# Weight sums by negation and accumulating loads, and a two-level down product in two more chunks

## The chip, the core and the metric

The kernel runs on one core of a Trainium2 chip. The core has a matrix engine (TensorE, PE in the profile; PEld are its weight loads), a vector engine (VectorE, DVE), a scalar engine (ScalarE, ACT), a general engine (GpSimd, POOL) and a queue engine (SyncE, SP) that only issues transfers here. Transfers that SP and POOL issue run on 16 DMA engines. The metric is the device time of one execution in microseconds (us); lower is better.

## The reference

An attention block without softmax, followed by a mixture of four experts. For each of 8 batches and 8 heads of width 64, `kv = k^T v`, then `q kv`, then each row is divided by its root mean square and multiplied by `g_norm`. The heads are put side by side, which gives x with 4608 rows (tokens) of 512. Then:

```
p = domain_probs / (domain_probs.sum(-1, keepdims=True) + 1e-09)
for e in range(4):
    h = np.maximum(x @ w1[e], 0.0)          # 4608x512 @ 512x1024
    out += p[:, e:e + 1] * (h @ w2[e])      # 4608x1024 @ 1024x512
```

Everything is float32. Nearly all of the work is in the eight large products of the experts.

## The kernel before

**Tiling.** The tokens are cut into 9 chunks of 512: eight are the first 512 rows of each batch, the ninth holds the remaining 64 rows of all eight. The loops run over expert e (0 to 3) and within it over chunk c (0 to 8); stage s = 9 e + c. Each stage has an *up* product (x by w1, then ReLU) and a *down* product (hidden by w2).

**Fewer products.** Both products use the scheme of Strassen and Winograd: a matrix is cut into 2 by 2 blocks, and 7 block products replace 8, at the price of sums of blocks before and after. `up` applies it twice, one inside the other: 7 outer by 7 inner products of 128-wide blocks. It does so for every stage but the first. For the down product there are two forms:

- `down` (line 1077) applies the scheme once: 2 token halves, 7 products, and 4 blocks of depth for each, 256 columns wide (matmul at line 1095). A product is scaled by the token's probability and merged into an accumulator straight from PSUM (lines 1042, 1049).
- `down_deep` (line 1117) applies it twice: 7 outer by 7 inner products, 2 blocks of depth each, 128 columns wide (matmul at line 1170). It needs sums of the hidden blocks (three for each outer product, through `combine`, line 360), evictions and sums of the inner products (lines 1198, 1206), and sums of the outer ones (line 1236) before the merge.

A float32 matmul shows as two instructions. Expert 0 uses `down` throughout. Experts 1 to 3 use `down_deep` for chunks 0 to 7, and `down` for chunk 8.

**Weights.** Both weights of an expert are loaded as four 512 KB blocks each, of 128 partitions by 1024. `weights_1` (line 417) forms four more blocks by sums, 5 = 21 + 4, 6 = 5 - 1, 7 = 1 - 21, 3 = 2 - 6, and then for each of the 7 outer factors four inner sums of 128 by 256 (kept in `w1y`). `weights_2` (line 466) forms 5 = 12 - 1, 6 = 3 - 5, 7 = 3 - 12, 4 = 2 - 6; its `inner` makes four sums for each outer factor into `w2y`. These serve `down_deep` only. The seven `w2y` slots are memory that the attention block used before (`kv`, `kvbd`, `x_rem`), and the profile shows them under those names. A sum is one `tensor_tensor` at line 360, on DVE or on POOL, whichever the planner picks.

**Memory.** Whole blocks of 128 by 1024 (weights, hidden blocks, products, accumulators) live in 29 slots named `big`, with 4 more (`small` in the profile) once the attention block is done. PSUM has 8 banks: `u1` and `u2` for up, `db` and `ab` for down.

**Order.** Nothing is left to a run-time scheduler. Every operation is handed to a planner with a key, in units of one stage, and a cost for each engine that may run it; the planner (`Plan.layout`, line 81) simulates the engines with these costs and gives each engine a fixed list. PE and SP take the first operation that is ready in order of key; the others take the ready one that is due first. A slot is given out when the planner starts the operation that first writes it. A transfer that POOL issues is taken to land 5.5 us after its issue (line 175). `port` (lines 129, 176) keeps `combine` sums from being planned on DVE and POOL at the same time. For the next expert's weights the keys are given at lines 1292 to 1294, where s is the last stage of the expert: loads of w1 from s, its inner sums from s + 0.3 and its four block sums at s + 0.55 to s + 0.8; loads of w2 from s + 0.6, its block sums from s + 1.0, its inner sums from s + 1.3. The up of stage s has keys s to s + 1, its down s + 1.2 to s + 2.2.

The results of experts 1 to 3 are added to the output in memory by transfers that accumulate, which POOL issues (line 1065); the last stage reads the output back instead.

Of the kernel before, what the change touches and what calls it, by code (L numbers as in the profile page):

```python
# [10 lines left out]
ALU = mybir.AluOpType  # L11
# [23 lines left out]
class Plan:  # L35
# [45 lines left out]
    def layout(self, slots, later, idle, idle_banks, idle_until):  # L81
# [51 lines left out]
        while left:  # L133
# [4 lines left out]
            for eng in todo:  # L138
                if busy[eng] > t:
                    continue  # L140
                pending = todo[eng]
                while pending and pending[0].start is not None:
                    pending.pop(0)
                if not pending:
                    continue
                reach = pending[0].key + self.REACH[eng]
                best = None
                for op in pending:
                    if op.key > reach:
                        break  # L150
                    if op.start is not None:
                        continue
                    if best is not None and op.due >= best.due:
                        continue
                    when = ready(op, eng)
                    if when is None:
                        continue
                    if when > t:
                        heapq.heappush(wake, when)
                        continue  # L160
                    best = op
                    if eng in ("PE", "SP"):
                        break
                if best is not None:
                    op = best
                    op.start, op.eng = t, eng
                    if eng == "SP":
                        busy[eng] = t + op.cost[eng]
                        bus = max(bus, t + 1.5) + op.kb / 215.0
                        op.end = bus + 0.5  # L170
                        lanes = lanes[1:] + [op.end]
                    else:
                        op.end = busy[eng] = t + op.cost[eng]
                        if op.kb:
                            op.end += 5.5
                    if op.port:
                        port = op.end
                        heapq.heappush(wake, port)
                    for b in op.outs:
                        if b.kind is not None and b.slot is None:  # L180
                            free[b.kind].sort()
                            b.slot = free[b.kind].pop(0)[1]
                            b.ap = slots[b.kind][b.slot]
                    for b in op.bufs:
                        b.left -= 1
                        if b.left == 0 and b.kind is not None:
                            end = max(o.end for o in [op] + b.readers + b.writers) + self.CROSS
                            free[b.kind].append((end, b.slot))
                            live[b.kind] -= 1
                            ended[b.kind] = max(end, ended.get(b.kind, 0.0))  # L190
                            for rule in [r for r in later if not any(live.get(k) for k in r[0])]:
                                later.remove(rule)
                                end = max(ended[k] for k in rule[0])
                                for ap in rule[2]:
                                    free.setdefault(rule[1], []).append((end, len(slots[rule[1]])))
                                    slots[rule[1]].append(ap)
                                heapq.heappush(wake, end)
                    heapq.heappush(wake, busy[eng])
                    heapq.heappush(wake, op.end + self.SAME)
                    heapq.heappush(wake, op.end + self.CROSS)  # L200
                    order.append(op)
                    left -= 1
                    moved = True
                if eng == "PE" and busy[eng] <= t and 1.6 <= t and front < idle_until:
                    kind, spare = next((
                        (k, f) for k in idle_banks for f in free[k] if f[0] <= t
                    ), (None, None))
                    if spare is not None:
                        op = Op(front, {"PE": 0.23}, None, (), (), 0, False)
                        op.start, op.eng, op.end = t, eng, t + 0.23  # L210
                        op.fn = lambda eng, bank=slots[kind][spare[1]]: idle(bank)
                        busy[eng] = op.end
                        free[kind].remove(spare)
                        free[kind].append((op.end, spare[1]))
                        heapq.heappush(wake, op.end)
                        order.append(op)
                        moved = True
# [13 lines left out]
def kernel(  # L231
# [110 lines left out]
    def act(n):  # L342
        return {"ACT": 0.155 + 0.00088 * n}
# [69 lines left out]
    def w2_src(e, uh, dh):  # L413
        rows = moe_w2[e][uh * HF:(uh + 1) * HF, dh * HN:(dh + 1) * HN]
        return rows.rearrange("(kt p) d -> p kt d", p=P)

    def weights_1(e, key, step, need):

        f = {n: Buf("big", f"w1_{e}_{n}") for n in (1, 2, 21, 4, 5, 6, 7, 3)}
        corner = {}  # L420
        w1corner[e] = {}
        for i, (n, dh, uh) in enumerate(((1, 0, 0), (2, 1, 0), (21, 0, 1), (4, 1, 1))):
            corner[n] = Buf(None, f"w1c_{e}_{n}")
            w1corner[e][uh, dh] = f[n], corner[n]
            load(
                key + i * step, f[n],
                lambda n=n: f[n].ap[:].rearrange("p (k u) -> p k u", k=2),
                w1_src(e, dh, uh), 512, also=[corner[n]],
            )

        def form(k_, o, a, b, op):
            corner[o] = Buf(None, f"w1c_{e}_{o}")
            combine(
                k_, either(1024), lambda: f[o].ap[:], lambda: f[a].ap[:], lambda: f[b].ap[:], op,
                [f[a], f[b], corner[a], corner[b]], [f[o], corner[o]],
            )

        def sums():
            form(need + 0.25, 5, 21, 4, ALU.add)
            form(need + 0.26, 6, 5, 1, ALU.subtract)  # L440
            form(need + 0.5, 7, 1, 21, ALU.subtract)
            form(need + 0.5, 3, 2, 6, ALU.subtract)
            w1f[e] = {}
            for j, m in enumerate(OUTER):
                x, low, y = f[m], corner[m], Buf("w1y", f"w1y_{e}_{m}")
                parts = {}
                for n, (uq, kt) in ((1, (0, 0)), (2, (0, 1)), (7, (1, 0)), (4, (1, 1))):
                    parts[n] = (
                        [x, low] if n == 7 else [x],
                        lambda x=x, uq=uq, kt=kt: two(x.ap[:])[:, kt, uq * HN:(uq + 1) * HN],  # L450
                    )
                for n, at in ((5, 0), (6, 1), (3, 2)):
                    parts[n] = ([y], lambda y=y, at=at: y.ap[:, at * HN:(at + 1) * HN])
                for o, a, b, op in (
                    (5, 7, 4, ALU.add), (7, 1, 7, ALU.subtract), (6, 5, 1, ALU.subtract),
                    (3, 2, 6, ALU.subtract),
                ):
                    combine(
                        need + j / 7, either(HN), parts[o][1], parts[a][1], parts[b][1], op,
                        parts[a][0] + parts[b][0], [low] if o == 7 else [y],  # L460
                    )
                w1f[e][m] = parts

        return sums

    def weights_2(e, key, step, deep):
# [9 lines left out]
        def form(k_, o, a, b, op):  # L476
            combine(
                k_, either(1024), lambda: f[o].ap[:], lambda: f[a].ap[:], lambda: f[b].ap[:], op,
                [f[a], f[b]], [f[o]],
            )  # L480

        form(key + 4 * step, 5, 12, 1, ALU.subtract)
        form(key + 5 * step, 6, 3, 5, ALU.subtract)
        form(key + 6 * step, 7, 3, 12, ALU.subtract)
        form(key + 7 * step, 4, 2, 6, ALU.subtract)
        w2f[e] = f

        def inner():
# [798 lines left out]
    for e in range(E):  # L1287
        for c in range(NCH):
# [1 line left out]
            if e == 0 and c + 1 < B:  # L1290
                attention(c + 1, s - 0.1, 0.8, s + 0.5)
            if e + 1 < E and c == NCH - 1:
                weights_1(e + 1, s + 0.0, 0.12, s + 0.3)()
                inner[e + 1] = weights_2(e + 1, s + 0.6, 0.1, s + 1.3)
            if s + 1 < E * NCH:
                if e == 0 and c + 1 < NCH:
                    x_views[s + 1] = x_forms(c + 1, s + 0.7)
# [3 lines left out]
                up(s, e, x_views.pop(s))  # L1301
            if c == 0 and e:
                inner[e]()
            if e and c < NCH - 1:
                if not primed:
                    banks = [Buf("ab", f"prime{i}") for i in range(2)]

# [66 lines left out]
```

## Time and profile before

| | us |
|---|---|
| median of 4 runs | 1730.39 (1729.66 to 1730.51) |
| the profiled execution | 1730.5 |
| its span | 1728.7 |
| L881, `up`, matrix instructions on `xf` and `big`: 3104, mean | 0.275 |
| L1095, `down`: instructions on `db`: 1120, mean | 0.381 |
| plain loads of the expert weights, 512 KB each: issue to landing | 4.8 (median) |
| accumulating output transfers, 256 KB each: issue to landing | 5.6 (median) |

Matrix instructions overlap, so the mean duration of one is longer than the interval between two; the interval is read from the chain of waits, where a run of n instructions has its length beside it. The last stage of expert 1 is s = 17; its down runs between 907 and 956 us, and expert 2 repeats the pattern 396 us later.

### The profile page before, as it was taken

The page shows a single profiled execution, that of the slowest core. Times are in us where ns is not written, and L with a number is a line of the kernel's source. Part 1 is how long each engine was busy: PE and PEld are TensorE (multiplying, and loading weights), DVE is VectorE, ACT ScalarE, POOL GpSimd, SP SyncE. Part 2 cuts the span into 40 slices and gives each one's busy share as a digit, 9 for nine tenths or more (in the row PEclk, how much of TensorE's full clock was granted, in tenths as well). Part 3 has the DMA queues.
Part 4 walks back from the last instruction along what each step waited for, and adds up shares of the span by engine and source line. Part 5 has one row for each costly group of instructions (what it writes and reads, how often), then busy time and mean ns, then how long its engine had stood idle before and what let it go on. Part 6 is the DMA issues. An engine that isn't in the chain of part 4 may idle for free.

```text
span 1728.7 us, 38444 instructions
## 1 busy us (share of the span) xinstructions
PE 1719.3 (99%) x15334; PEld 1651.5 (96%) x15334; DVE 1225.9 (71%) x1969; ACT 938.4 (54%) x2300; POOL 614.2 (36%) x560
## 2 busy tenths in 40 slices
PE   9999999999999999999999999999999999999998
PEld 7699999999999999999999999999999999999998
DVE  4755655565676777777788877777788877777774
ACT  3354544454444565656555556666655566565652
POOL 2421322133334333333345333333345333333331
PEclk9999999999999999999999999999999999999999
DMA  9756444633433243444465344444475344444432
GB/s 239 219 161 193 151 121 132 193 135 125 151 128 100 94 115 104 115 107 112 130 187 111 99 110 111 111 111 110 108 208 113 98 111 111 111 111 103 114 103 49
DMA packets 148596, 220.94 MB, mean 128 GB/s; under 512 B 49600, under 2 KB 90816, under 8 KB 148416
## 3 DMA queue, kind: packets, MB, share of 16 engines
q1 hardware_dynamic: 133312, 191.21, 35.2%
q0 software_dynamic: 15104, 27.27, 10.7%
q8 instruction: 120, 1.97, 0.5%
q14 instruction: 60, 0.49, 0.1%
HBM read 145.30 MB, written 73.14 MB: 126 GB/s over the span
## 4 chain that ended last, share of the span: by engine, by line
PE 99%; POOL 0%; DVE 0%; ACT 0%; issue 0%; POOLq 0%
PE u L881 45%; PE db L1170 19%; PE db L1095 14%; PE ab L1170 12%; PE ab L1095 2%; PE u L968 2%; PE ab L634 1%; PE ab L678 1%; PE ab L620 1%; PE ab L1323 1%; PE ab L660 1%; PE u L1095 1%; PE db L660 0%; POOL rt L551 0%; PE ab L722 0%; PE ab L704 0%
## 5 line engine op out<-in xcount | busy, mean ns | idle before, releaser
L360 DVE TENSOR_TENSOR big<-big,big 128x1024 f32<-128x1024 f32 (+1 forms) x450 | 442.3, 996 | 34.9 <-ACT big L864 23.8
L881 PE MATMUL u<-xf,big 128*128 128x128 f32 x3104 | 453.0, 275 | 0.0
L881 PEld LDWEIGHTS u<-xf,big 128*128 128x128 f32 x3104 | 401.3, 192 | 2.2
L881 PE MATMUL u<-xf,w1y 128*128 128x128 f32 x2652 | 389.6, 275 | 0.0
L908 DVE TENSOR_TENSOR big<-u,snap 128x256 f32<-128x256 f32 x430 | 181.4, 422 | 234.3 <-PE u L881 175.5
L881 PEld LDWEIGHTS u<-xf,w1y 128*128 128x128 f32 x2652 | 343.4, 192 | 2.2
L900 ACT ACTIVATE snap<-u 128x256 f32<-128x256 f32 x490 | 187.8, 383 | 251.5 <-PE u L881 212.7
L1095 PE MATMUL db<-big,big 128*128 128x256 f32 x1120 | 265.3, 381 | 2.1 <-DVE big L560 2.1
L1095 PEld LDWEIGHTS db<-big,big 128*128 128x128 f32 x1120 | 203.5, 191 | 24.8 <-DVE big L560 2.3
L900 ACT ACTIVATE big<-u 128x256 f32<-128x256 f32 x430 | 164.7, 383 | 110.6 <-PE u L881 74.5
L360 POOL TENSOR_TENSOR big<-big,big 128x256 f32<-128x256 f32 (+1 forms) x138 | 170.1, 1239 | 132.4 <-DVE big L360 49.4
L1170 PE MATMUL db<-big,big 128*128 128x128 f32 x1056 | 146.7, 275 | 0.0
L864 ACT ACTIVATE big<-big 128x1024 f32<-128x1024 f32 x128 | 134.5, 1050 | 2.7 <-POOL big L360 1.5
L1170 PEld LDWEIGHTS db<-big,big 128*128 128x128 f32 x1056 | 132.1, 192 | 0.1
L1236 POOL TENSOR_TENSOR big<-big 128x512 f32<-128x512 f32 x26 | 33.0, 1269 | 269.0 <-DVE big L360 263.9
L1198 ACT ACTIVATE snap<-db 128x256 f32<-128x256 f32 x192 | 68.4, 356 | 100.0 <-PE db L1170 95.1
L360 POOL TENSOR_TENSOR big<-big 128x512 f32<-128x512 f32 (+1 forms) x57 | 70.3, 1233 | 126.8 <-DVE big L360 102.6
L1170 PE MATMUL db<-kv,big 128*128 128x128 f32 x804 | 114.6, 275 | 0.0
L1065 POOL DMA_DIRECT2D out_dram<-big x100 | 91.2, 988 | 48.2 <-ACT snap L1198 22.8
L900 ACT ACTIVATE u<-u 128x256 f32<-128x256 f32 x245 | 90.9, 371 | 28.1 <-PE u L881 8.0
L1170 PEld LDWEIGHTS db<-kv,big 128*128 128x128 f32 x804 | 102.1, 192 | 0.1
L1206 DVE TENSOR_TENSOR big<-ab,snap 128x256 f32<-128x256 f32 x140 | 59.1, 422 | 56.8 <-ACT snap L1198 31.8
(218 smaller groups left out, 2686.6 us busy)
## 6 DMA issues: line engine op xcount, KB each, us to landing
xf<-x SPq DMA_DIRECT2D x108, 512.0 KB, 3.6
out_dram<-big POOLq DMA_DIRECT2D x84, 256.0 KB, 5.6
xf<-x_h SPq DMA_DIRECT2D x81, 256.0 KB, 3.0
xf<-x SPq DMA_DIRECT2D x81, 256.0 KB, 3.1
x<-xf SPq DMA_DIRECT2D x36, 512.0 KB, 6.6
big<-in_moe_w_dram SPq DMA_DIRECT2D x25, 512.0 KB, 4.8
small<-in_q_dram SPq DMA_DIRECT2D x72, 128.0 KB, 4.9
kv<-in_k_dram SPq DMA_DIRECT2D x30, 288.0 KB, 4.8
```

Of the source, the lines that this page charges most:

```text
L360: lambda eng: adder(eng).tensor_tensor(out=out_(), in0=a(), in1=b(), op=op),
L864: lambda eng: nc.scalar.activation(out=b.ap[:], in_=b.ap[:], func=ACT.Relu),
L881: nc.tensor.matmul(ps.ap[:, u * P:(u + 1) * P], lhsT=w1f[e][m][mm][1]()[:, u * P:(u + 1) * P], rhs=views[m][mm][1](), start=(mm in (1, 5) ...
L900: lambda eng: nc.scalar.activation(out=where(), in_=ps.ap[:, 0:HN], func=ACT.Copy),
L908: lambda eng: nc.vector.tensor_tensor(out=block(whole, a, t), in0=src.ap[:, 0:HN], in1=add_.ap[:], op=ALU.add),
L968: nc.tensor.matmul(bank.ap[:], lhsT=two(w.ap[:])[:, kt, ut * P:(ut + 1) * P], rhs=two(xh[dh].ap[:])[:, kt, :], start=(dh == kt == 0), stop ...
L1065: nc.gpsimd.dma_start(out=dst, in_=cell(i)[parts, :], accum_op=ALU.add)
L1095: nc.tensor.matmul(ps.ap[:, 0:HN], lhsT=four(h[m])[:, kt // 2, t, kt % 2, :], rhs=w2f[e][m].ap[:, kt * HN:(kt + 1) * HN], start=(m in (1, ...
L1170: nc.tensor.matmul(ps.ap[:, o * P:(o + 1) * P], lhsT=b.ap[:, col:col + P], rhs=w2q[e][m][mm][1]()[:, kt, :], start=(mm in (1, 5) and o == ...
L1198: lambda eng: nc.scalar.activation(out=where(), in_=group_of(ps.ap), func=ACT.Copy),
L1206: lambda eng: nc.vector.tensor_tensor(out=cell(tq, dq), in0=group_of(src.ap), in1=group_of(add_.ap), op=ALU.add,),
L1236: lambda eng: adder(eng).tensor_tensor(out=whole(to), in0=whole(a), in1=whole(b), op=ALU.add),
```

## The change

Three things are done.

1. For experts 1 to 3, two of the four block sums of w1 (7 and 3) and all four of w2 (5, 6, 7, 4) are made in another way. ACT writes the negated block into the new slot (a Copy with scale -1, 128 by 1024), and then a transfer that POOL issues adds the other operand to it, straight from the weights in DRAM: 7 = -21 + block 1, 3 = -6 + block 2; 5 = -1 + block 12, 6 = -5 + block 3, 7 = -12 + block 3, 4 = -6 + block 2. The w1 transfers read 256 rows of 2 KB, the w2 ones 512 rows of 1 KB. Expert 0 keeps the sums. The sums 5 and 6 of w1 stay as they were.
2. The last chunks of experts 1 and 2 (stages 17 and 26) use `down_deep` in place of `down`. Only expert 0 and the very last stage keep `down`.
3. The planner takes these 512 KB transfers to land 9.0 us after their issue. The keys for the next expert's weights move: inner sums of w1 from s + 0.3 to s + 0.6 (its block sums with them), loads of w2 from s + 0.6 to s + 1.0 (its block sums with them), inner sums of w2 from s + 1.3 to s + 1.45. These keys hold for all three changes of expert.

```diff
@@ Plan.layout
                         if op.kb:
-                            op.end += 5.5
+                            op.end += 9.0 if op.kb == 512 else 5.5
@@ new, after w2_src
+    def subtract_from(key, to, view, a, src, reads, writes):
+
+        plan.add(
+            key, act(2 * NT),
+            lambda eng: nc.scalar.activation(
+                out=to.ap[:], in_=a.ap[:], func=ACT.Copy, scale=-1.0),
+            reads=reads, writes=[to],
+        )
+        plan.add(
+            key, {"POOL": 1.0},
+            lambda eng: nc.gpsimd.dma_start(out=view(to.ap), in_=src, accum_op=ALU.add),
+            reads=[to], writes=writes, kb=512,
+        )
@@ weights_1
+        def from_dram(k_, o, a, dh, uh):
+            corner[o] = Buf(None, f"w1c_{e}_{o}")
+            subtract_from(
+                k_, f[o], lambda ap: ap[:].rearrange("p (k u) -> p k u", k=2), f[a],
+                w1_src(e, dh, uh), [f[a], corner[a]], [f[o], corner[o]],
+            )
+
         def sums():
             form(need + 0.25, 5, 21, 4, ALU.add)
             form(need + 0.26, 6, 5, 1, ALU.subtract)
-            form(need + 0.5, 7, 1, 21, ALU.subtract)
-            form(need + 0.5, 3, 2, 6, ALU.subtract)
+            if e:
+                from_dram(need + 0.5, 7, 21, 0, 0)
+                from_dram(need + 0.5, 3, 6, 1, 0)
+            else:
+                form(need + 0.5, 7, 1, 21, ALU.subtract)
+                form(need + 0.5, 3, 2, 6, ALU.subtract)
@@ weights_2
-        form(key + 4 * step, 5, 12, 1, ALU.subtract)
-        form(key + 5 * step, 6, 3, 5, ALU.subtract)
-        form(key + 6 * step, 7, 3, 12, ALU.subtract)
-        form(key + 7 * step, 4, 2, 6, ALU.subtract)
+        for i, o, b, uh, dh, a in (
+            (4, 5, 12, 0, 1, 1), (5, 6, 3, 1, 1, 5), (6, 7, 3, 1, 1, 12), (7, 4, 2, 1, 0, 6)
+        ):
+            if e:
+                subtract_from(
+                    key + i * step, f[o], lambda ap: ap[:].rearrange("p (k d) -> p k d", k=4),
+                    f[a], w2_src(e, uh, dh), [f[a]], [f[o]],
+                )
+            else:
+                form(key + i * step, o, b, a, ALU.subtract)
@@ the loop over experts and chunks
             if e + 1 < E and c == NCH - 1:
-                weights_1(e + 1, s + 0.0, 0.12, s + 0.3)()
-                inner[e + 1] = weights_2(e + 1, s + 0.6, 0.1, s + 1.3)
+                weights_1(e + 1, s + 0.0, 0.12, s + 0.6)()
+                inner[e + 1] = weights_2(e + 1, s + 1.0, 0.1, s + 1.45)
...
-            if e and c < NCH - 1:
+            if e and s < E * NCH - 1:
```

## The prediction

> **What bounds the kernel now.** I read the page's shares first, then its chain of waits, then the list of waits on TensorE (PE), and last the windows around one change of expert.
>
> ```profile
> span 1728.7 us, 38444 instructions
> PE 1719.3 (99%) x15334; PEld 1651.5 (96%) x15334; DVE 1225.9 (71%) x1969; ACT 938.4 (54%) x2300; POOL 614.2 (36%) x560
> PEclk9999999999999999999999999999999999999999
> ...
> PE 99%; POOL 0%; DVE 0%; ACT 0%; issue 0%; POOLq 0%
> ```
>
> PE is busy for 99% of the span, at the full clock, and is 99% of the chain that ended last. A busy PE could still hide waits, so the second view asks who waited on it:
>
> ```profile
> PE db L1095 <- DVE big L560: 2.1, 1, 2.1
> PE ab L1323 <- POOL ident masks.py:199: 1.4, 1, 1.4
> PE u L881 <- ACT snap L900: 0.6, 1, 0.6
> PE u L881 <- ACT u L900: 0.5, 1, 0.5
> PE ab L678 <- ACT big L686: 0.3, 1, 0.3
> ```
>
> This is the whole list, and all five fall in the first 100 us. So the time is the number of PE instructions times their pace. Nothing is won by relieving another engine unless PE work goes away.
>
> The pace, from the chain in order of time (start, us, what):
>
> ```profile
> 920.60 1.73 PE db L1095 x8
> 924.50 5.18 PE db L1095 x24
> ...
> 960.02 0.89 PE db L1170 x8
> 964.04 0.89 PE u L881 x8
> ```
>
> A 256-column instruction of the plain down takes 1.73/8 = 0.2163 us, a 128-column one of the two-level down 0.1116 (300 us of steady running hold 2689 instructions).
>
> The change of expert, in windows (length, PE, PEld, DVE, ACT, POOL busy, clock, DMA share, GB/s):
>
> ```profile
> 880.00:902.00 22.00, 22.00 (x200) 22.00 (x199) 20.04 (x30) 10.46 (x28) 10.48 (x8) 1.00 0.59 192
> 902.00:924.00 22.00, 22.00 (x179) 21.43 (x178) 17.32 (x29) 15.56 (x40) 13.74 (x13) 1.00 0.54 129
> 924.00:946.00 22.00, 22.00 (x139) 20.32 (x138) 18.89 (x27) 9.35 (x20) 9.85 (x13) 1.00 0.52 101
> 946.00:968.00 22.00, 22.00 (x175) 21.36 (x174) 18.94 (x31) 11.09 (x25) 11.93 (x14) 1.00 0.41 108
> ```
>
> VectorE (DVE) is busy 75.2 of 88 us (85%), in the first window 91%, and PE still loses nothing.
>
> **Part 1: two-level down in two chunks.** Plain down: 2 token halves x 7 products x 4 depth blocks x 2 passes = 112 instructions x 0.2163 = 24.2 us. Two-level: 7 x 7 products x 2 depth blocks x 2 passes = 196 x 0.1116 = 21.9 us. All of it lies on the path. Two chunks (s = 17 and 26): 2 x (24.2 - 21.9) = 4.7 us less.
>
> Beside it, each such chunk adds sums, by the page's groups (mean of one):
>
> ```profile
> L360 DVE TENSOR_TENSOR big<-big,big 128x1024 f32<-128x1024 f32 x264 | 350.0, 1330 | 33.9 <-ACT big L864 23.8 <-DMA big<-in_moe_w_dram 1.2 <-PE u L881 0.3
> L360 DVE TENSOR_TENSOR big<-big,big 128x256 f32<-128x256 f32 x186 | 95.2, 523 | 1.1 <-POOL big L360 0.3
> L360 DVE TENSOR_TENSOR big<-big 128x512 f32<-128x512 f32 x89 | 88.6, 1009 | 0.0
> L1236 DVE TENSOR_TENSOR big<-big,big 128x512 f32<-128x512 f32 x98 | 71.4, 729 | 3.0
> L864 ACT ACTIVATE big<-big 128x1024 f32<-128x1024 f32 x128 | 134.5, 1050 | 2.7 <-POOL big L360 1.5 <-DVE big L360 1.2
> L1065 POOL DMA_DIRECT2D out_dram<-big x100 | 91.2, 988 | 48.2 <-ACT snap L1198 22.8 <-ACT big L1042 16.8 <-DVE big L360 2.0
> ```
>
> Seven 512-wide forms of h (7.1 us), fourteen 256-wide (7.3), the PSUM totals (six at 0.42, two at 0.29: 3.1), seven 512-wide product sums (5.1), less six merges at 0.48 (2.9): 19.7 us of DVE if GpSimd (POOL) takes none. ACT gains 20 evictions of 0.26 to 0.38 us, 7.1.
>
> **Part 2: six weight sums per expert off DVE.** Out go 6 sums of 1.33 us = 8.0 us per change of expert (at most 2.4 each where POOL did them). In come 6 negations, which are ACT passes of the ReLU's shape (6 x 1.05 = 6.3 us), and 6 issues on POOL. Since PE waits for no DVE work here, part 2 alone is worth 0. It pays only as cover for part 1: DVE gets 19.7 - 8.0 = 11.7 us more at the second and third change of expert, 8.0 less at the first.
>
> ACT goes from 46.5 to 46.5 + 7.1 + 6.3 = 59.9 of 88 us (68%); queued behind a 1.05 us negation are the PSUM evictions, as behind a ReLU now, and PE waits for none of those. POOL's issue: the row has 0.99 us for 256 KB in 128 rows; the new ones carry 512 KB in 256 rows (w1) or 512 (w2). Bounds 0.99 (the row is mostly fixed cost) to 4 x 0.99; I take 1.5, nearer the fixed end since the 128 KB issues of that line are no cheaper. That is 9 us of POOL per change (6 to 24), on 46 of 88. Behind a waiting issue stand POOL's own sums and the output's accumulating issues, for which nothing but DVE sums waits.
>
> **When the data lands.** The accumulating output takes 5.6 us from issue for 256 KB, 7.3 near 870 us where weights load too. Doubling the bytes: at least 7.3, at most 2 x 7.3 = 14.6; I take 9, as 128 KB took 4.3 to 4.6, so most is fixed. One step costs 1.05 + 9, about 10 us. In the second weight three steps follow each other (5, then 6, then 4). From the last plain load (key 18.3) to the first use of 6 (key 19.2) are 0.9 stages of 392 x 0.1116 = 43.7 us, 39 us for two steps (20) and four 256-wide sums (2.1); 4 is wanted at 19.77, 64 us for 30. The first weight's 3 has 0.47 stages, 20 us, for 10 + 2.1. Spare 8 us at the tightest, so 0 on the path.
>
> The queues that are moved past: SP issues the four plain loads of w2 0.4 stages later (880 to 893 us now), behind x loads that PE needs sooner. The accumulating queue used 10.7% of the span, 185 us of all 16 DMA engines, for 27.27 MB, 6.8 us per MB; 6 x 0.524 MB more is 21 us per change, on a mean share of 0.52 in these 88 us: 0.76. Not full, so 0.
>
> Here a page speaks. The Trainium skill, "DMA: Bandwidth & Descriptors", section "Anatomy of one DMA", fits a GpSimd-issued transfer as 2.0 us plus bytes over 436 GB/s: 3.2 us for 512 KB, and by it a step would be near 4.3 us and the chain of three 13. It gives 2.6 us for 256 KB where this trace shows 5.6, so it is not used.
>
> Against the change stands the Trainium skill, "SBUF — State Buffer", section "SBUF: two separate sides": the port pair shared by DVE and GpSimd is an exclusive lock, and descriptors of a GpSimd DMA cannot be written while DVE holds it in a two-port mode. This trace has 100 such issues among a DVE busy 71% of the time, at 0.80 to 1.22 us, so by the row an issue is held up by 0.3 us at most over its median, 6 x 0.3 = 1.8 us of POOL per change; by the rule each could wait out one 1.33 us sum, 8 us of POOL. Either fits beside POOL's 46 of 88, and the sum holds neither on the path.
>
> **Buffers.** The key numbers let me count 1024-wide buffers (33 slots) near key 18.5. Before: 7 of the new w1, 8 of the new w2, 7 old w2, 7 of h, 2 accumulators, 3 of the running up, 34 at the edge. After: 8, up to 8, 5, 5, 2, 3 and 5 for forms and products, up to 36, with the new w2 started 0.4 stages later. Tight both times; late is then a weight form that has until 19.2 or later. New waits: between 0 (the rows of before) and one 1.33 us sum at each of two changes; I take 0.4 in all, nearest the rows.
>
> **The sum.** 0 - 4.7 + 0.4 = -4.3 on the profiled execution's 1730.5 us (span 1728.7 and 1.8 around it; 0.1 above the median): 1726.2 us.
>
> **The rivals.**
> - *DVE becomes the bound (slower).* In 880 to 968 us DVE would need 75.2 + 11.7 = 86.9 of 88 us. The busiest window of before is 91%, which is 80.1 us: an excess of 6.8 at each of two changes, 1725.8 + 13.6 = 1739.4. If POOL takes a third of the 11.7 (its share of the 512-wide forms now: 52 of 141), the excess is 2.9 each, 1731.6. For: 85% already. Against: the sums of the inner weights can slide; 858 to 1012 us has DVE at 128 of 154. It decides (over +0.2%) from 4.1 us each, when POOL takes under 2.7.
> - *Slots run out.* A product that finds no buffer holds PE until one comes free, on the scale of one up group, 28 x 0.1116 = 3.1 us. Two missing at two changes: up to 12.5 us; one at each, 6.2: 1732. For: 34 and 36 against 33. Against: no wait at 34.
> - *Loads land late.* An in-order DVE that reaches a sum before its data blocks evictions behind it. At 14.6 + 1.5 the first weight's 3 needs 19 of 20 us, so it decides only beyond; 5 us at each of three changes would give 1741. For: the same queue carries four accumulating outputs per stage, and the DMA share is 0.78 in 858 to 880. Against: the spare.
> - *Half eaten:* any of these at half its smallest price leaves about 1728, no change. That the change does not do what it says can be set aside: the product counts follow from the loops.
>
> **How the numbers follow.** About 0.2% (3.5 us) is what a measurement tells from no change. Forecast 0.54 (own range 1725.2 to 1727.0); DVE bound 0.20 (same 0.06, slower 0.14); slots 0.14 (0.07, 0.07); late loads 0.07 (all slower), a half-eaten gain 0.05 (all same). Faster 0.54, same 0.18, slower 0.28. The range goes from 1725.0 to 1737: above it lie the upper ends of the three rivals, about 0.12.
>
> **What would show it.** Right: 224 instructions of L1095 replaced by 392 of L1170, PE's list of waits still empty after 100 us, DVE at or under 90% in 860 to 1010. Wrong: PE waiting on DVE, ACT or DMA near 900 to 970 and 1300 to 1370, or a PE busy time down by 4.7 with the span not following. A landing over 16 us of the new loads would break the working of the chain.

## The result and the profile after

The changed kernel takes 1728.15 us (median of 41 runs, 1727.07 to 1729.40) beside 1730.47 us for the kernel before (61 runs, 1729.66 to 1730.92): a ratio of 0.9987, 95% interval 0.9983 to 0.9992. It is 2.3 us faster, where the two chunks should have saved 4.7. That is a gain beyond its interval, but less than the 0.2% that the forecast named. The profiled execution took 1728.7 us, its span is 1726.9. Behind the new functions the lines have moved by 31: the up product is L912, the one-level down L1126, the two-level down L1201, its evictions L1229, the output transfers L1096. The new negation is L421 and the new accumulating load L427.

The page, shares of the engines and of the chain that ended last:

```profile
span 1726.9 us, 38938 instructions
PE 1715.4 (99%) x15502; PEld 1653.0 (96%) x15502; DVE 1221.3 (71%) x2001; ACT 965.4 (56%) x2358; POOL 634.5 (37%) x588
...
PE 98%; DMA 1%; POOL 0%; ACT 0%; issue 0%; DVE 0%; ACTq 0%; POOLq 0%
```

There are 168 more PE instructions, which is 392 of one kind for 224 of the other. A new share stands in the chain: 1% DMA. The list of waits of PE (us in total, times, longest) says where:

```profile
PE db L1126 <- DVE big L591: 2.1, 1, 2.1
PE ab L1354 <- POOL ident masks.py:199: 1.4, 1, 1.4
PE ab L1201 <- ACT big L1229: 1.3, 1, 1.3
PE ab L1201 <- ACT small L1229: 0.9, 1, 0.9
PE u L912 <- ACT snap L931: 0.6, 1, 0.6
PE u L912 <- ACT u L931: 0.5, 1, 0.5
PE ab L709 <- ACT big L717: 0.2, 1, 0.2
```

The third and fourth lines are new, one at each of the last two changes of expert. The chain in order of time (start, us, what) around the first of them:

```profile
908.13 0.46 PE u L912 x4
...
909.90 0.41 ACT big L1073
...
910.34 0.25 POOL out_dram L1096
910.59 0.36 issue
910.95 9.58 DMA out_dram<-big
...
920.63 0.39 ACT big L1229
921.03 0.04 issue
921.07 1.16 PE ab L1201 x8
```

It is read from the bottom. PE starts a two-level product at 921.07 once ACT has emptied its bank (L1229). ACT could not, because the slot that it writes was still being read by a transfer to the output, issued at 910.34 and landed 9.58 us after 910.95. That transfer carries the accumulator of stage 16; the slot is given next to the products of stage 17. The planner took a landing of 5.5 us for it. The second place has the same chain with 9.18 us. ACT's own timeline shows the wait:

```profile
918.00 0.38 ACT L931 ACTIVATE snap<-u 128x256 f32<-128x256 f32 x1 [0.90 <-PE u L912]
920.63 0.38 ACT L1229 ACTIVATE big<-ab 128x256 f32<-128x256 f32 x1 [2.25 <-DMA out_dram<-big]
```

The windows (PE, PEld, DVE, ACT, POOL busy, clock, DMA share, GB/s):

```profile
880.00:902.00 22.00, 22.00 (x199) 22.00 (x199) 20.33 (x30) 13.70 (x33) 11.06 (x13) 1.00 0.66 167
902.00:924.00 22.00, 20.68 (x185) 20.49 (x185) 16.27 (x28) 14.50 (x37) 11.90 (x12) 1.00 0.89 218
924.00:946.00 22.00, 22.00 (x200) 22.00 (x199) 18.23 (x36) 13.49 (x31) 10.19 (x11) 1.00 0.68 139
946.00:968.00 22.00, 22.00 (x200) 22.00 (x199) 17.20 (x30) 14.69 (x38) 12.88 (x12) 1.00 0.44 116
```

Where DVE is busiest (20.33) PE loses nothing. Where the DMA share is highest (0.89, before it was 0.54) PE runs 185 instructions in place of 200.

### The profile page after: what moved, and what is told of

It is laid out like the page before. It is cut to its first block, busy times and chain, and to the rows that moved or that the text cites. A ratio compares the mean times of both kernels' runs of the same rounds, so it can differ in the third digit from the quotient of the medians.

```text
span 1726.9 us, 38938 instructions
## 1 busy us (share of the span) xinstructions
PE 1715.4 (99%) x15502; PEld 1653.0 (96%) x15502; DVE 1221.3 (71%) x2001; ACT 965.4 (56%) x2358; POOL 634.5 (37%) x588
## 3 DMA queue, kind: packets, MB, share of 16 engines
q1 hardware_dynamic: 133312, 191.21, 35.3%
q0 software_dynamic: 23072, 36.71, 14.3%
## 4 chain that ended last, share of the span: by engine, by line
PE 98%; DMA 1%; POOL 0%; ACT 0%; issue 0%; DVE 0%; ACTq 0%; POOLq 0%
PE u L912 44%; PE db L1201 20%; PE db L1126 13%; PE ab L1201 13%; PE u L999 2%; PE ab L665 1%; PE ab L709 1%; PE ab L651 1%; PE ab L1354 1%; PE ab L691 1%; PE u L1126 1%; DMA out_dram<-big 1%; DMA out_dram<-small 1%; PE ab L1126 0%; PE db L691 0%; POOL rt L582 0%
## 5 line engine op out<-in xcount | busy, mean ns | idle before, releaser
L360 DVE TENSOR_TENSOR big<-big,big 128x1024 f32<-128x1024 f32 (+1 forms) x485 | 462.3, 970 | 38.9 <-ACT big L895 23.9
L912 PE MATMUL u<-xf,big 128*128 128x128 f32 x3248 | 472.2, 275 | 0.0
L912 PEld LDWEIGHTS u<-xf,big 128*128 128x128 f32 x3248 | 418.2, 192 | 1.7
L912 PE MATMUL u<-xf,w1y 128*128 128x128 f32 x2652 | 389.8, 275 | 0.0
L939 DVE TENSOR_TENSOR big<-u,snap 128x256 f32<-128x256 f32 x454 | 191.6, 422 | 242.5 <-PE u L912 175.9
L912 PEld LDWEIGHTS u<-xf,w1y 128*128 128x128 f32 x2652 | 343.1, 192 | 1.8
L360 POOL TENSOR_TENSOR big<-big,big 128x256 f32<-128x256 f32 (+1 forms) x148 | 192.2, 1313 | 153.9 <-DVE big L360 80.6
L1126 PE MATMUL db<-big,big 128*128 128x256 f32 x1032 | 245.0, 381 | 2.1 <-DVE big L591 2.1
L1126 PEld LDWEIGHTS db<-big,big 128*128 128x128 f32 x1032 | 187.0, 191 | 22.7 <-DVE big L591 2.3
L1201 PE MATMUL db<-big,big 128*128 128x128 f32 x1000 | 139.9, 275 | 0.0
L895 ACT ACTIVATE big<-big 128x1024 f32<-128x1024 f32 x131 | 137.7, 1051 | 3.3 <-DVE big L360 3.2
L1201 PE MATMUL db<-kv,big 128*128 128x128 f32 x940 | 137.1, 275 | 0.0
L360 POOL TENSOR_TENSOR big<-big 128x512 f32<-128x512 f32 (+1 forms) x67 | 84.3, 1260 | 133.4 <-DVE big L360 108.6
L1229 ACT ACTIVATE snap<-db 128x256 f32<-128x256 f32 x208 | 74.1, 356 | 99.3 <-PE db L1201 94.7
L1201 PEld LDWEIGHTS db<-big,big 128*128 128x128 f32 x1000 | 125.6, 192 | 0.1
L1201 PEld LDWEIGHTS db<-kv,big 128*128 128x128 f32 x940 | 120.8, 192 | 0.0
L1096 POOL DMA_DIRECT2D out_dram<-big x96 | 86.7, 1018 | 45.0 <-ACT big L1073 23.8
## 6 DMA issues: line engine op xcount, KB each, us to landing
small<-in_q_dram SPq DMA_DIRECT2D x72, 128.0 KB, 4.7
```

The costliest lines, as they stand in the source:

```text
L360: lambda eng: adder(eng).tensor_tensor(out=out_(), in0=a(), in1=b(), op=op),
L895: lambda eng: nc.scalar.activation(out=b.ap[:], in_=b.ap[:], func=ACT.Relu),
L912: nc.tensor.matmul(ps.ap[:, u * P:(u + 1) * P], lhsT=w1f[e][m][mm][1]()[:, u * P:(u + 1) * P], rhs=views[m][mm][1](), start=(mm in (1, 5) ...
L939: lambda eng: nc.vector.tensor_tensor(out=block(whole, a, t), in0=src.ap[:, 0:HN], in1=add_.ap[:], op=ALU.add),
L1096: nc.gpsimd.dma_start(out=dst, in_=cell(i)[parts, :], accum_op=ALU.add)
L1126: nc.tensor.matmul(ps.ap[:, 0:HN], lhsT=four(h[m])[:, kt // 2, t, kt % 2, :], rhs=w2f[e][m].ap[:, kt * HN:(kt + 1) * HN], start=(m in (1, ...
```

## The experiments

Two theories stood at the start. *Landing*: the output transfers land later than planned, and the wait for their slots costs the missing 2.4 us. *Busy engines*: the added sums and negations make DVE or ACT the engine that PE waits for.

**The output transfers shortened.** Only the bytes that move change; every engine keeps its order.

```diff
-nc.gpsimd.dma_start(out=dst, in_=cell(i)[parts, :], accum_op=ALU.add)
+nc.gpsimd.dma_start(out=dst[:, 0:P if s in (16, 25) else DM],
+                    in_=cell(i)[parts, 0:P if s in (16, 25) else DM], accum_op=ALU.add)
```

> The accumulating output transfers of stages 16 and 25 carry 128 of their 512 columns, so three quarters of those two chunks' results of experts 1 and 2 are left out of the output; every instruction and its order on every engine stay as in the changed kernel. Landing theory (of the 4.7 us that the two chunks save, about 2.4 is lost because the scalar engine, at line 1229, writes a product into a slot whose output transfer lands 9.2 to 9.6 us after its issue, where the planner took 5.5): the landing falls towards 5 us, the two waits of PE near 920 and 1315 us are gone, and the time is 1725.8. Busy-engine theory (the vector engine and the scalar engine, loaded by the added sums and negations, are what PE waits for): nothing changes, 1728.1.

Measured: 1725.88 us, ratio 0.9975 (0.9964 to 0.9985). Both waits are gone, and the slowest landing of the four transfers near 910 us is 7.0 us in place of 9.6. A busy PE does not show short waits, so instructions in the two stretches are the better measure. Of the changed kernel:

```profile
858.00:1012.00 154.00, 152.68 (x1367) 1.00 0.63 152
1254.00:1408.00 154.00, 153.10 (x1371) 1.00 0.62 152
```

and of this one:

```profile
858.00:1012.00 154.00, 154.00 (x1382) 1.00 0.62 149
1254.00:1408.00 154.00, 154.00 (x1382) 1.00 0.62 149
```

15 and 11 instructions more, 26 x 0.1116 = 2.9 us. The last product ends at 1724.14 us before, at 1722.30 in the changed kernel and at 1719.39 here: 4.75 us saved, of which the changed kernel's profiled execution keeps 1.84. The landing theory holds; the busy-engine theory falls, since all sums and negations are still there.

**The loads beside them shortened.** First the accumulating loads of the weights, then the four plain loads of the second weight, to a quarter of their bytes each, again with every order kept.

```diff
-nc.gpsimd.dma_start(out=view(to.ap), in_=src, accum_op=ALU.add)
+nc.gpsimd.dma_start(out=view(to.ap)[:, :, 0:HN // 4], in_=src[:, :, 0:HN // 4], accum_op=ALU.add)
```

> The 18 accumulating loads of the weights carry a quarter of their bytes (64 of 256 columns, 128 KB), so three quarters of six weight sums per expert are left as the negated block alone; the order of every engine stays as in the changed kernel. Landing theory with crowding (the output transfer lands late because a 512 KB accumulating load that was issued 3 us before it shares the queue and the DMA engines): the landing of the output transfers near 910 and 1306 us falls from 9.2 to 9.6 towards 7 us, both waits shrink below 0.5, and the time is 1726 to 1726.5. Landing theory without crowding by these loads (it is the plain loads or the output itself): landing and waits stay, 1728.1. Busy-engine theory: stay, 1728.1.

```diff
 load(key + i * step, f[n],
-    lambda n=n: f[n].ap[:].rearrange("p (k d) -> p k d", k=4), w2_src(e, uh, dh), 512)
+    lambda n=n: f[n].ap[:].rearrange("p (k d) -> p k d", k=4)[:, :, 0:HN if e == 0 else HN // 4],
+    w2_src(e, uh, dh)[:, :, 0:HN if e == 0 else HN // 4], 512)
```

> In the changed kernel, the four plain loads of the second weight of experts 1 to 3 carry a quarter of their columns (128 KB in place of 512), so three quarters of those weights are stale data and the results of experts 1 to 3 are not the reference's; the order of every engine stays. If these loads, which the moved keys put beside the output transfers, are what makes those land late: the landing near 911 us falls from 9.6 to 7 or less, PE's two waits go and the time is 1725.8 to 1726.3. If it is the accumulating queue itself: about as with the shortened accumulating loads, 1727.2, or 1728.1.

| | time, us | ratio to before | landing of the four output transfers, min/median/max: 906 to 920 us | 1302 to 1316 us |
|---|---|---|---|---|
| changed kernel | 1728.15 | 0.9987 | 7.4/7.9/9.6 | 7.4/7.9/9.2 |
| accumulating loads short | 1727.24 | 0.9982 (0.9973 to 0.9991) | 7.7/7.8/8.9 | 6.9/7.3/8.5 |
| plain loads short | 1726.45 (1725.61 to 1728.63) | 0.9977 (0.9968 to 0.9986) | 7.0/7.3/8.4 | 7.5/8.3/9.9 |

Each takes part of the loss away, 0.9 and 1.7 us of the 2.3 between 1728.15 and the 1725.88 above, and neither brings the median landing under 7 us; neither time is the one that its theory gave. The profile of the third row is its slowest execution (1728.63; 0.7 us of it is a wait for an input of the attention part): one change is clean (landing 8.4 at most, 1379 instructions), the other waits (9.9, 1365). In all six stretches of the table PE's wait is the slowest landing less about 8.3 us: 1.6 us for 9.9, 1.3 for 9.6, 0.9 for 9.2, 0.7 for 8.9, 0.2 for 8.5 and, by PE's busy time, 0.1 for 8.4; with the 7.0 and 7.3 of the shortened outputs there is none. So the output transfers have 8.3 us to land before PE pays, where the planner counts on 5.5. By the times both kinds of load crowd the output transfers; how they share the delay is not settled.

**Each part alone.** The sums without the down, then the down without the sums (on the kernel before, with its keys).

```diff
-if e and s < E * NCH - 1:
+if e and c < NCH - 1:
```

> The weight sums by negation and accumulating loads with the moved keys, but the one-level down in the last chunk of experts 1 and 2 as before. Prediction's step (relief of the vector engine is worth 0 by itself): no wait of PE after 100 us, same PE instructions as the kernel before, 1730.5. Crowding rival (the accumulating loads delay things by themselves, whatever the down does): PE waits appear at the changes of expert, 1732 to 1733.

Measured: 1730.61 us, ratio 1.0000 (0.9991 to 1.0009). Relief of DVE is worth nothing by itself, though the output transfers land as late here (7.6/8.2/8.9 near 912 us, 7.7/8.5/9.2 near 1309). The slots go to negations here, which wait 2.5 and 2.4 us for them on ACT, and PE does not wait for those: its list has one new line after 100 us, 0.2 us for DVE near 1330, and the second stretch has 1273 instructions in place of 1277.

```diff
-if e and c < NCH - 1:
+if e and s < E * NCH - 1:
```

> The kernel before with nothing but the two-level down in the last chunk of experts 1 and 2; weight sums and keys as before. Cover theory (the prediction: without the six sums taken off it the vector engine would need 75.2 + 19.7 of 88 us and PE would wait for it): PE waits on DVE near 900 to 970 and 1300 to 1370 us, 1731 to 1740. Rival (the vector engine had room, and the sums need no cover): 1725.8 to 1728.

Measured: 1733.14 us, ratio 1.0016 (1.0007 to 1.0024), slower than before. New lines in the waits of PE (L881 is up here, L908 its sums out of PSUM), and the windows:

```profile
PE u L881 <- DVE big L908: 2.6, 3, 1.0
...
PE u L881 <- ACT u L900: 1.1, 3, 0.5
PE ab L1170 <- ACT ab L1198: 0.6, 1, 0.6
```

```profile
924.00:946.00 22.00, 22.00 (x197) 21.84 (x197) 16.39 (x31) 11.31 (x30) 8.68 (x9) 1.00 0.31 85
946.00:968.00 22.00, 21.12 (x187) 20.73 (x186) 20.89 (x36) 13.55 (x34) 7.78 (x7) 1.00 0.27 92
```

DVE is busy 20.89 of 22 us (95%) in the second window, and the chain that ended last runs there on DVE alone for 13 us, most of it sums of line 360:

```profile
940.39 2.48 PE u L881 x20
943.38 1.25 DVE small L360
...
954.57 1.21 DVE big L360
956.51 1.16 PE u L881 x8
```

In this list PE waits for DVE. It is not the load of the whole change that does it: in 858 to 1012 us DVE is busy 125.6 us here, 125.5 in the run with the short output transfers, where PE loses nothing, and 127.2 in the run with the old keys below, where it loses 4 instructions. The first window also shows a PE that is busy for all of its 22 us with 3 of 200 instructions missing.

**Which part of the cover: the sums or the keys.** The changed kernel with plain sums again and the moved keys, and the changed kernel with the old keys.

```diff
-            if e:
+            if False:
                 from_dram(need + 0.5, 7, 21, 0, 0)
...
-            if e:
+            if False:
                 subtract_from(
```

> The changed kernel with the six weight sums as sums on the vector engine or GpSimd again; the two-level down and the moved keys stay. Cover by the sums (what holds the vector engine's load down is that six sums leave it): as slow as the two-level down alone, 1732 to 1734. Cover by the keys (what helps is that the weight sums come later): near the changed kernel, 1727 to 1729.

```diff
-weights_1(e + 1, s + 0.0, 0.12, s + 0.6)()
-inner[e + 1] = weights_2(e + 1, s + 1.0, 0.1, s + 1.45)
+weights_1(e + 1, s + 0.0, 0.12, s + 0.3)()
+inner[e + 1] = weights_2(e + 1, s + 0.6, 0.1, s + 1.3)
```

> The changed kernel with the keys of the kernel before (inner sums of w1 from s + 0.3, loads of w2 from s + 0.6, inner sums of w2 from s + 1.3). Cover by the sums: near the changed kernel, 1727 to 1729. Cover by the keys: 1731 to 1734. If the late output transfers of the changed kernel come from the plain loads of the second weight, which the moved keys put into 898 to 912 us beside them, the landing of the output transfers near 910 us is back at 6 to 7 us here and the time is 1725.8 to 1727.

Measured: 1733.73 us, ratio 1.0020 (1.0011 to 1.0029), without the loads from DRAM; 1726.84 us, ratio 0.9980 (0.9971 to 0.9989), with them and the old keys. With the same keys, then, the kernel whose six sums have left is faster each time: by 5.6 us with the moved keys (1733.73 and 1728.15) and by 6.3 with the old ones (1733.14, the run above, and 1726.84). That speaks for the sums and against the keys as the cover. But the 1733.73 is not a price of the sums alone. No wait of PE names DVE in that run; the longest two are 1.4 and 1.2 us for ACT (L1229), one at each change, and behind both the chain has a late output transfer again, here by way of a sum on POOL and a ReLU on ACT (L895). At the first change:

```profile
910.23 8.55 DMA out_dram<-small
...
918.94 2.36 POOL small L360
...
921.60 1.05 ACT small L895
922.65 0.28 ACT snap L1229
```

The moved keys cost 1.3 us where the sums have left: with the old keys the plain loads of the second weight come earlier (the DMA share is 0.84 in 880 to 902 us and 0.56 in 902 to 924), the transfers land in time, and PE has no new wait. The output transfers near 910 us with the old keys:

```profile
L1096 POOL DMA_DIRECT2D out_dram<-big x3: 874/909/1208, 910.2 to 918.7; - x3
...
DMA to landing us min/median/max: 4.0/5.4/6.0
```

**The planner told the truth.** One figure: the landing that the planner takes for the output transfers.

```diff
-op.end += 9.0 if op.kb == 512 else 5.5
+op.end += 9.0 if op.kb == 512 else 9.0      # 11.0 in the second run
```

> The changed kernel, with the planner told that the accumulating output transfers too land 9.0 us after their issue, in place of 5.5; nothing is left out. The planner's whole order changes from expert 1 on. Landing theory: the slot of an accumulator is given out later, so no eviction meets a transfer in flight; PE's two waits near 920 and 1315 us go and the time is 1725.8 to 1726.3. Rival (slots are too few, so that a planner that knows the true landing can only move the wait to another place): 1727.5 to 1729, with PE waits or missing instructions elsewhere in 900 to 960 and 1300 to 1360.

> The same with 11.0 us, above every landing seen for an output transfer (9.6). Landing theory: as with 9.0, 1725.8 to 1726.3. Rival (too few slots): a longer assumed landing costs more, 1727.5 to 1730.

Measured: 1733.11 us, ratio 1.0016 (1.0007 to 1.0025), with 9.0; 1726.63 us, ratio 0.9978 (0.9968 to 0.9987), with 11.0. Neither theory had foreseen both. With 11.0 there is no new wait and each stretch has 1378 of 1382 instructions. The output transfers near 910 us still take up to 8.1 us, at a DMA share of 0.94 in 902 to 924 us, higher than the 0.89 of the changed kernel; so the mean share of a window does not give the landing. DVE is busy 20.61 of 22 us in 946 to 968 and PE loses nothing there. With 9.0 the first change loses 15 instructions and the second 51:

```profile
1298.00:1320.00 22.00, 20.40 (x177) 19.78 (x177) 18.16 (x32) 11.41 (x30) 10.17 (x10) 1.00 0.93 224
1320.00:1342.00 22.00, 20.35 (x179) 20.11 (x180) 17.60 (x30) 14.93 (x36) 14.69 (x10) 1.00 0.60 125
```

PE's timeline there shows no transfer behind the waits: PE has only products of the down to run, two of the groups waiting for an eviction on ACT, and then waits for DVE:

```profile
1318.22 0.68 PE L1201 MATMUL db<-kv,small 128*128 128x128 f32 x4 [0.56 <-ACT snap L1229]
...
1319.91 0.68 PE L1201 MATMUL db<-small,small 128*128 128x128 f32 x4 [0.56 <-ACT snap L1229]
...
1322.69 0.71 PE L912 MATMUL u<-xf,w1y 128*128 128x128 f32 x4 [1.65 <-DVE big L939]
```

It is a list in which no up product stands beside the down for a while.

**Both remedies.**

```diff
-op.end += 9.0 if op.kb == 512 else 5.5
+op.end += 9.0 if op.kb == 512 else 11.0
-weights_1(e + 1, s + 0.0, 0.12, s + 0.6)()
-inner[e + 1] = weights_2(e + 1, s + 1.0, 0.1, s + 1.45)
+weights_1(e + 1, s + 0.0, 0.12, s + 0.3)()
+inner[e + 1] = weights_2(e + 1, s + 0.6, 0.1, s + 1.3)
```

> The keys of the kernel before together with a planned landing of 11.0 us for the output transfers; nothing is left out. Each alone took the waits away. If what is left of each (0.8 to 1.0 us over 1725.8) is short waits that the landing plan and the keys each cause, the two together give 1725.8 to 1727. If the planner's orders fall out one way or the other with any change of its figures, as 9.0 did, it can also be 1727 to 1733.

Measured: 1735.29 us, ratio 1.0028 (1.0017 to 1.0038), above both of its forecasts. The remedies do not add; the waits are those of the 9.0 run (PE for the snapshots of L1229, 2.8 us in six waits, and 1.1 for DVE), at both changes, and the output transfers land in 6.1 us in the middle. So four kernels with the same work, in which PE waits for no late landing, take 1726.6, 1726.8, 1733.1 and 1735.3 us. That the planner's order makes the difference follows from the code, which is otherwise the same; which choice in it does was not tried and stays open. In all four the six sums have left DVE, and two of them are as slow as the runs that kept the sums. So taking the sums away is not enough, and it is not shown that no order with the sums in place could keep the 4.7 us. Both 11.0 alone and the old keys alone beat the changed kernel, by 1.5 and 1.3 us, and the kernel before by 3.8 and 3.6.

## Why the prediction was right or wrong

- *What bounds the kernel.* Right: PE's instructions times their pace. The saving of 4.7 us is confirmed by the run with the short output transfers, 1725.88 us, and by 4.75 us at the last product. The 224 instructions did become 392.
- *Part 2 alone is worth 0 and pays as cover.* The first is right: 1.0000 alone. The second holds for the two pairs that were measured, 5.6 and 6.3 us; that every order needs the cover is not shown.
- *New waits: between 0 and one 1.33 us sum at each change, 0.4 taken.* This is the term that failed. It measured 2.3 us in the median and 2.9 in the profiled execution, around its upper end of 2.66 and six times the value taken. The forecast of 1726.2 was 2 us too fast for this alone, and the time fell to the forecast's case of a half-eaten gain (about 1728, given 0.05). The time lies outside the forecast's own 1725.2 to 1727.0, and inside 1725.0 to 1737 only because that range was drawn wide for the rivals, so it does not speak for the sum. The sign of being wrong came as named: PE waits on ACT, with a DMA behind it, near 920 and 1316 us.
- *Why it failed.* The bound came from the engines' waits, and the section on buffers let a late buffer fall on a weight form, which had time. It fell on the eviction of a product of the down. It needed the rival "slots run out" and the rival "loads land late" together, and for another transfer than the one that was counted. The prediction read the landing of the output at 870 us as 7.3 and used it only to price the weight loads. It gave these 8 us to spare and set the crowded queue to 0 with a mean DMA share of 0.76. The share was 0.89 in the window where four output transfers, three of the plain loads and one of the accumulating ones fell together, and the transfers short of time were the outputs: the two-level down takes their slots next, 8.3 us after the issue, and they landed after up to 9.6.
- *The landing of the new loads.* Taken as 9 us after an issue of 1.5 (range 7.3 to 14.6). Measured in the changed kernel, with the issues in ns min/median/max:

```profile
L427 POOL DMA_DIRECT2D big<-in_moe_w_dram x15: 1202/1288/1416, 495.4 to 1336.6; - x15
...
DMA to landing us min/median/max: 5.6/6.1/10.4
```

  The line shows 15 of the 18 issues; the three into `small` took 1.20 to 1.87 us, and the landing is that of all 18. The middle is below the range's lower end, and PE waits for none of them. The Trainium skill, "DMA: Bandwidth & Descriptors", section "Anatomy of one DMA", gives 3.2 us for 512 KB as an estimate from its fit; the measured middle is about twice that, so the measurement decides.
- *The issues on POOL.* The prediction let each new issue wait out one 1.33 us sum of DVE by the rule on the shared port pair. That rule, as it quotes it, is for a two-port mode of DVE, and nothing here shows that the sums are in one. The new issues took 1.20 to 1.87 us with 1.5 taken, so none shows a wait of that length.
- *The load on DVE.* Wrong in size: 11.7 us more were expected on it at each of the last two changes. In 858 to 1012 us DVE went from 128.0 to 123.7 and POOL from 72.1 to 79.1. Of the 18 sums that left, the large ones on POOL fell from 65 to 52 and those on DVE only from 356 to 351: most of the room was made on POOL. Of the 42 small sums at line 360 that the two-level down added, POOL took 13 and DVE 29. Yet DVE's sums of these two widths took 331.6 us in all, beside 329.6 before, because the mean of one fell (256 wide: 518 to 495 ns). So the mean of a row was not the price of one more; why it fell was not tried. ACT was expected at 59.9 of 88 us and measured 13.70 + 14.50 + 13.49 + 14.69 = 56.4.
- *The rival "DVE becomes the bound".* It did not happen in the changed kernel, and in the down alone, without its cover, PE waited for DVE, at 1733.1 us. The 1731.6 to 1739.4 that were worked out for it had the cover in place, so its price was set too high, with the load on DVE.

## What to carry to other kernels

When a change gives an operation a buffer that was free before, ask what releases that buffer, and look up the landing of that transfer in the stretch where it will happen, not its median over the run. Count instructions in a window beside the busy time: a busy engine can hide waits, and here 15 and 11 missing instructions at the two changes were the whole loss. A list schedule made from assumed times can answer a truer figure with a worse order, so a planner's constant is to be measured at more than one value before it is believed.

## What the runs showed of the hardware

- A 512 KB accumulating load from memory into SBUF landed 5.6 to 10.4 us after its issue, in the middle 6.1, not much later than a 256 KB accumulating output transfer (5.9 in the middle from the `big` slots). Shortened to 128 KB, the loads landed in 3.0/3.7/5.1 us. The output transfers, of 128 and 256 KB, landed in 3.6 to 9.6 us in one execution, so a median over the run says little of one stretch.
- In this kernel's mix an accumulating transfer uses the DMA engines about twice as long for a byte: the accumulating queue took 14.3% of the span for 36.71 MB (6.7 us of 16 engines per MB), the plain one 35.3% for 191.21 MB (3.2).
- Cutting an output transfer to a quarter (64 KB) brought its slowest landing near 910 us only from 9.6 to 7.0 us; that was enough, since a landing of 8.4 cost 0.1 us and one of 8.9 a wait of 0.7.
